# Queries and keys with 14 tokens a partition, turned in 64x64 blocks; values in four transfers a unit

## The chip, the cores and the metric

One Trainium2 chip, one of its cores. The metric is the device time of one execution in microseconds. Three runs of the kernel before took 314.25, 314.24 and 313.91 us, a median of 314.24. Engines: TensorE (PE, with PEld for its weight loads), VectorE (DVE), ScalarE (ACT), GpSimd (POOL) and SyncE (SP, which only issues transfers here). POOL issues transfers too, and those convert float32 to bfloat16 on the way.

## The reference

```python
batch, n_heads, seq, head_dim = (8, 12, 448, 64)          # q, k, v: float32, 0.1 * randn
N, D, E, S_per_e, F = (3584, 768, 8, 4, 1024)             # phi [768, 32], w1 [8, 768, 1024], w2 [8, 1024, 768]

def _attn_ref(q, k, v):
    scale = 1.0 / np.sqrt(q.shape[-1])
    scores = scale * np.matmul(q, k.transpose(0, 1, 3, 2))
    m = np.max(scores, axis=-1, keepdims=True)
    e = np.exp(scores - m)
    attn = e / (np.sum(e, axis=-1, keepdims=True) + np.exp(-m) + 1e-09)
    return np.matmul(attn, v)

def _moe_ref(x, phi, w1, w2):
    logits = x @ phi
    d = np.exp(logits - logits.max(0, keepdims=True))
    d /= d.sum(0, keepdims=True) + 1e-09
    slot_input = (d.T @ x).reshape(E, S_per_e, D)
    for e in range(E):
        slot_out[e] = np.maximum(slot_input[e] @ w1[e], 0.0) @ w2[e]
    c = np.exp(logits - logits.max(1, keepdims=True))
    c /= c.sum(1, keepdims=True) + 1e-09
    return c @ slot_out.reshape(n_slots, D)
```

The attention's output, heads side by side, is the x of the second function: 3,584 tokens of 768. The maximum m cancels out of the attention but for the 1e-09, so any value will do for it that is used in all three places alike.

## The kernel before, in words

A **unit** is two batches and two heads: 24 units (`U`), `HP` = 6 head pairs for each of `BP` = 4 batch pairs. Each unit has seven **steps** (`TB` = 7), one for every 64 (`P`) query rows of both batches. The program is written out by hand: functions are entered into a plan under a step (unit x 7 + an offset) and a place in it, and the loop at the end runs each step's places in the order small, scores, mid, value, transposed scores, end, load. `SCH` holds the offsets and places of a unit's parts, `MIX` and `FIN` those of the second function, `WAT` and `LATE` those of the weight loads. Each engine works through its instructions in that order.

Parts of a unit, with their lines:

- `load_qk` (L171, through `load`, L164): queries and keys come by four POOL transfers a unit, one for each tensor and batch, two units ahead. A batch takes 64 partitions; partition p holds tokens 7p to 7p + 6 of both heads, so a run in memory is 7 x 64 floats, 1,792 bytes. `SCH['qk']` puts them at steps 1, 2 and 6.
- `load_v` (L177): values in the same layout, float32, two SP transfers a unit (by POOL in the first unit); `stage_V` (L387) casts them to bfloat16 on POOL.
- `stage_T` (L302): PE turns queries and keys so that the head dimension lies on the partitions: 28 transposes (2 tensors x 7 tokens x 2 heads), each with 128 partitions and 64 columns in and 64 x 128 out (L326). DVE copies all of it from PSUM at once (L327). For the first unit they go a batch at a time in blocks of 64 x 64 (L315), 28 for each batch, with a DVE copy for each (L317); `T0` says when the second batch comes, `T1` when the second unit's turn comes.
- `stage_S` (L330): scores for one step, four matmuls of 64 x 64 by 448 columns, or two with 128 output rows where the step also holds attention-times-value work; DVE takes the row maxima (L347) into `M`.
- `stage_MT` (L349): the maxima are turned (L354), copied by ACT (L357), their exponential goes into `em` (L360), and POOL spreads them (L364). `MT0` is its place in the first unit.
- `stage_ST` (L370), `LAG` = 11 steps later: the maxima (L375) and the transposed scores (L380) are added up in PSUM; ACT takes the exponential (L384).
- `stage_AV` (L393, L409): the exponentials times the values, 65 columns with one of ones for the sum; `stage_AVout` (ACT, L419), `stage_den` (POOL, L425), `stage_N` (reciprocal on DVE, L443; products on POOL, L432), `stage_X` (turned for the second function, L483 and a copy, L485).

The second function runs in between, once per batch pair (`mixture`), and finishes after the last unit. `gate_T` (L593) turns the gates and copies them on ACT into `cT` (L598, L600), in the order of the output rows. Weights come by POOL: 48 transfers of 64 rows (L195, placed by `WAT`), and eight late ones (L204) into rooms that the attention's buffers leave free (`LATE` adds steps to the earliest ones).

PSUM has four slots of two banks each; `slot` hands them out by a rule of when each is due to be free. Waits between engines follow from which buffers are read and written.

Of the kernel before, what the change touches and what calls it, by code (L numbers as in the profile page):

```python
# [10 lines left out]
BF16 = mybir.dt.bfloat16  # L11
# [5 lines left out]
P = 64  # L17
LAG = 11
AV0 = (15, 15, 16, 17, 18, 19, 19)
SCH = {'T': (6, 'value'), 'qk': ((2, 'load'), (1, 'mid'), (6, 'end'), (6, 'value')), 'MT': (6, 'load'), 'V': (13, 'mid'), 'v': ((14, 'load'), (17, 'end')), 'AVout': (19, 'mid'), 'N': ((23, 'value'), (23, 'small')), 'X': (27, 'end'), 'mix': (28, ''), 'den': (19, 'load'), 'lp': (29, 'value'), 'last': (21, 'load'), 'Xlast': (24, 'value'), 'k1': (20, 'mid'), 'k2': (30, 'value'), 'k3': (32, 'small'), 'k4': (34, 'load'), 'Xprev': (25, 'value'), 'T0': (1, 'mid'), 'T1': (4, 'value'), 'Vlast': (12, 'end'), 'MT0': (7, 'mid')}  # L20
MIX = {'logits': (0, 'end'), 'slot_max': (5, 'load'), 'slot_exp': (5, 'load'), 'gate_logits': (6, 'value'), 'gate_max': (6, 'value'), 'slots_T': (7, 'mid'), 'gate_exp': (7, 'value'), 'slot_sum': (13, 'small'), 'slot_in': (8, 'load'), 'gate_T': (13, 'end')}
FIN = {'merge_prev': (0, 'load'), 'logits': (1, 'load'), 'slot_max': (2, 'mid'), 'slot_exp': (2, 'value'), 'merge_max': (2, 'value'), 'slots_T': (3, 'mid'), 'slot_sum': (3, 'load'), 'merge_acc': (4, 'small'), 'slot_in': (4, 'end'), 'merge_sum': (5, 'end'), 'experts_in': (8, 'load'), 'gate_logits': (8, 'load'), 'gate_max': (9, 'small'), 'gate_exp': (10, 'load'), 'experts_hidden': (10, 'end')}
# [8 lines left out]
def kernel(  # L31
# [26 lines left out]
    G = E // 4  # L58
    scale = 1.0 / (D ** 0.5)

    ctx.enter_context(tc.manual_schedule())
    gdma = nc.gpsimd.dma_start

    const = ctx.enter_context(tc.tile_pool(name="const", bufs=1))
    small = ctx.enter_context(tc.tile_pool(name="small", bufs=2))
    psum = ctx.enter_context(tc.tile_pool(name="psum", bufs=1, space=PSUM))

    HW = (KC // 2) * F  # L70
# [817 lines left out]
```

## Time and profile before

| what | us |
|---|---|
| median of three runs | 314.24 |
| the profiled execution | 314.96 |
| its span, first to last instruction | 313.2 |
| PE, DVE, ACT, POOL busy in it | 271.0, 251.5, 209.2, 198.5 |
| DMA queue of POOL (36.69 MB), share of 16 engines' span | 70.6% |
| DMA queues of SP (21.57 MB) | 20.1% |
| granted TensorE clock, mean | 0.955 |

Busy time is the sum of what an engine executed, waiting left out. Lines of groups read: line, engine, operation, output<-input, shapes, count | busy us, mean ns of one | idle us of the engine just before them, with the work that ended it. Lines of a timeline read: start, duration, engine, line, operation, shapes, count, and in brackets the idle time before it and what ended that; "issue" is a wait for nothing that the profile shows. Groups of transfers: 112 KB each for queries and keys (96 of them, 4.4 and 4.6 us from issue to landing), 224 KB for values (46 from SP, 5.2 us), 384 KB for weights (48, 5.9 us), 768 KB for late weights (8, 8.9 us).

### The profile page before, as it was taken

The numbers are of one execution on the slowest core, as the hardware profiler recorded it, in microseconds if no ns is written. First come the engines' busy times: TensorE is split into PE (matmuls) and PEld (weight loads), VectorE is DVE, ScalarE is ACT, GpSimd is POOL, SyncE is SP. The second block draws the span as 40 slices with busy tenths as digits, with TensorE's granted clock in tenths as the row PEclk, the third lists the DMA queues.
The fourth block names the chain that finished last, engine by engine and source line by source line (L and its number), as shares of the span: only waits on it lengthen the run. The fifth ranks groups of instructions, "written<-read, shape, count | busy, mean of one in ns | idle before, by whom it ended". The sixth has DMA issues, their size and how long they took to land.

```text
span 313.2 us, 13694 instructions
## 1 busy us (share of the span) xinstructions
PE 271.0 (87%) x6080; PEld 153.6 (49%) x6080; DVE 251.5 (80%) x324; ACT 209.2 (67%) x306; POOL 198.5 (63%) x342
## 2 busy tenths in 40 slices
PE   3689899999989999998999989999989987987660
PEld 2235555655545555655555545555555553542110
DVE  2998889999979889998999889999979627328560
ACT  1127778878777888876787768787958884225351
POOL 8965877788867777798677866798756452100000
PEclk9999999999999999999999999999999999996555
DMA  6999899999989979999899889799987689936997
GB/s 89 170 166 204 164 178 171 201 179 175 176 160 178 212 136 184 190 178 176 151 201 194 164 146 200 128 207 185 196 169 162 137 143 188 210 74 268 421 425 294
DMA packets 29258, 59.12 MB, mean 189 GB/s; under 512 B 4272, under 2 KB 23216, under 8 KB 29200
## 3 DMA queue, kind: packets, MB, share of 16 engines
q0 software_dynamic: 19728, 36.69, 70.6%
q1 hardware_dynamic: 9472, 21.57, 20.1%
q8 instruction: 47, 0.77, 1.0%
q14 instruction: 11, 0.09, 0.1%
HBM read 83.46 MB, written 11.01 MB: 302 GB/s over the span
## 4 chain that ended last, share of the span: by engine, by line
PE 53%; DVE 11%; ACT 10%; DMA 9%; POOL 9%; issue 5%; ACTq 0%; POOLq 0%; DVEq 0%; SPq 0%
PE ps L409 13%; PE ps L340 11%; PE ps L375 10%; PE ps L380 7%; ACT block L384 7%; PE ps L326 5%; DVE m_sb L347 5%; DMA block<-in_moe_w_dram 4%; POOL block L167 3%; DMA out_dram<-wres 3%; PE ps L483 2%; DMA block<-in_q_dram 2%; PE ps L823 2%; DVE block L327 2%; POOL block L432 2%
## 5 line engine op out<-in xcount | busy, mean ns | idle before, releaser
L347 DVE TENSOR_REDUCE m_sb<-ps 128x2 bf16<-128x896 f32 x168 | 179.3, 1088 | 12.6 <-PE ps L340 6.0
L384 ACT ACTIVATE block<-ps 128x896 bf16<-128x896 f32 x168 | 153.5, 918 | 51.5 <-PE ps L380 44.3
L409 PE MATMUL ps<-block 64*128 64x65 bf16 (+1 forms) x2688 | 76.3, 192 | 2.1 <-issue 1.7
L409 PEld LDWEIGHTS <-block 64*128 64x128 bf16 (+1 forms) x2688 | 66.8, 97 | 20.7 <-issue 3.7
L375 PE MATMUL ps<-block 64*64 64x448 bf16 x672 | 70.0, 369 | 2.6 <-DVE acc L495 0.9
L340 PE MATMUL ps<-block 64*64 64x448 bf16 (+1 forms) x452 | 65.2, 387 | 6.2 <-DVE block L317 1.9
L380 PE MATMUL ps<-block 64*64 64x448 bf16 x672 | 66.4, 353 | 0.0
L340 PEld LDWEIGHTS <-block 64*64 64x64 bf16 (+1 forms) x452 | 23.0, 103 | 51.6 <-issue 39.8
L432 POOL TENSOR_TENSOR block<-block,rec 128x384 bf16<-128x384 f32 x46 | 37.3, 836 | 8.7 <-DVE rec L443 7.0
L375 PEld LDWEIGHTS <-block 64*64 64x64 bf16 x672 | 26.8, 106 | 13.3 <-issue 9.8
L167 POOL DMA_DIRECT2D block<-in_q_dram x48 | 30.6, 639 | 2.6 <-PE ps L340 1.8
L167 POOL DMA_DIRECT2D block<-in_k_dram x48 | 30.4, 636 | 1.9 <-PE ps L326 1.9
L364 POOL TENSOR_TENSOR block<-mt,base 128x512 bf16<-128x512 bf16 x23 | 24.2, 1054 | 6.1 <-ACT mt L357 5.9
L327 DVE COPY block<-ps 128x1792 bf16<-128x1792 bf16 x23 | 24.9, 1083 | 3.3 <-PE ps L326 3.3
L326 PE MATMUL ps<-ident,block 128*64 128x128 bf16 x644 | 24.6, 228 | 2.9 <-issue 2.7
L326 PEld LDWEIGHTS <-block 128*64 128x64 bf16 x644 | 21.6, 115 | 10.5 <-issue 9.5
L195 POOL DMA_DIRECT2D wres<-in_moe_w_dram x48 | 26.6, 556 | 0.1
L425 POOL TENSOR_TENSOR den<-block,em 128x14 f32<-128x14 f32 x23 | 4.9, 212 | 33.8 <-ACT block L419 33.2
L380 PEld LDWEIGHTS <-block 64*64 64x64 bf16 x672 | 24.2, 108 | 0.3 <-issue 0.2
L389 POOL CAST block<-block 128x896 bf16<-128x896 f32 x24 | 22.4, 933 | 2.8 <-PE ps L409 1.5
L419 ACT COPY block<-ps 128x910 f32<-128x910 f32 x22 | 20.2, 918 | 2.1 <-POOL block L437 0.6
L832 DVE TENSOR_SCALAR wres<-ps,acc 128x768 f32<-128x768 f32 (+1 forms) x16 | 14.7, 941 | 7.5 <-PE ps L823 5.0
(130 smaller groups left out, 220.4 us busy)
## 6 DMA issues: line engine op xcount, KB each, us to landing
wres<-in_moe_w_dram POOLq DMA_DIRECT2D x48, 384.0 KB, 5.9
block<-in_v_dram SPq DMA_DIRECT2D x46, 224.0 KB, 5.2
out_dram<-wres SPq DMA_DIRECT2D x11, 768.0 KB, 5.4
block<-in_moe_w_dram POOLq DMA_DIRECT2D x8, 768.0 KB, 8.9
block<-in_q_dram POOLq DMA_DIRECT2D x48, 112.0 KB, 4.4
block<-in_k_dram POOLq DMA_DIRECT2D x48, 112.0 KB, 4.6
out_dram<-wres SPq DMA_DIRECT2D x5, 384.0 KB, 5.1
block<-in_v_dram POOLq DMA_DIRECT2D x2, 224.0 KB, 4.6
```

What stands on the lines that cost most here:

```text
L167: eng.dma_start(out=t_[ds(b * P, P), :, :], in_=src[bp * 2 + b, ds(hp * 2, 2)].rearrange("h (p t) d -> p h (t d)", t=TB))
L195: gdma(out=t_[rows, ts(half, HW)], in_=src[rows, ts(half, HW)])
L326: nc.tensor.transpose(o[ds(h * D, D)], r[:, h, ts(t, D)], ident)
L327: (nc.vector.tensor_copy if OPT["T"] == "dve" else nc.scalar.copy)(t_, ps[:, :, ds(0, N2)].rearrange("p i (b n) -> p i b n", b=2))
L340: nc.tensor.matmul(ps[rs, h, ds(0, S)], QT[u][hs, b, ds(o, 128 if wide else P)], KT[u][hs, b, :], start=True, stop=True)
L347: nc.vector.tensor_reduce(m, ps[:, :, ds(0, S)], axis=AX.X, op=ALU.max)
L364: (nc.vector if end_ else nc.gpsimd).tensor_tensor(md.rearrange("p (a r n) -> p a r n", a=4, r=2), mt.rearrange("p (r n) -> p r n", r=2).u ...
L375: nc.tensor.matmul(ps[ds(b * P, P), h, ds(0, S)], select[hs, b, :], MD[u][b][hs, :], start=True, stop=False)
L380: nc.tensor.matmul(ps[ds(b * P, P), h, ds(0, S)], KT[u][hs, b, part_of(b, t)], QT[u][hs, b, :], start=False, stop=True)
L384: nc.scalar.activation(et, ps[:, :, ds(0, S)], AF.Exp, scale=scale)
L409: nc.tensor.matmul(o, et[bs, h, ds(c * 128 + b * P if c < C3 else c * 128 * (1 - b), w)], V65[u][bs, h, t, ds(0, 65)], start=(t == 0 and h ...
L432: eng.tensor_tensor(xo[:, ds(b * C3, C3)].rearrange("p c h d -> p h c d"), av[:, b, ds(0, 2 * C3 * 65)].rearrange("p (h c e) -> p h c e", ...
```

## The change

Queries and keys: one transfer for each tensor and head, still four a unit. A head takes 64 partitions, 32 for each batch; a partition holds 14 tokens, a run of 3,584 bytes. `stage_T` then works on one head's 64 partitions at a time: 56 transposes of 64 x 64, alternating between the heads, for every unit but the first. In the first unit the heads come one after the other (a call for each), queries and keys in a PSUM slot of their own, with DVE copying the queries and ACT the keys; its scores go a head at a time too, over both batches.

The tokens of a 64-row block come in another order by this (even positions, then odd ones), so values are loaded in four transfers of 32 partitions, each with every second group of seven tokens, and `gate_T` puts the output rows back in order with one ACT copy more. The plan's places, the weight loads' places and `LATE` are other ones: among them `T0` from step 1 to 0, `MT0` from (7, mid) to (5, small), `V` from (13, mid) to (13, end), the value loads a step earlier, `den` from step 19 to 20, `last` and `Xlast` a step earlier, one weight load moved from step 17 to 166.

```diff
-SCH = {..., 'V': (13, 'mid'), 'v': ((14, 'load'), (17, 'end')), ..., 'N': ((23, 'value'), (23, 'small')), ..., 'den': (19, 'load'), ..., 'last': (21, 'load'), 'Xlast': (24, 'value'), ..., 'T0': (1, 'mid'), 'T1': (4, 'value'), ..., 'MT0': (7, 'mid')}
+SCH = {..., 'V': (13, 'end'), 'v': ((13, 'load'), (16, 'end')), ..., 'N': ((23, 'small'), (23, 'small')), ..., 'den': (20, 'load'), ..., 'last': (20, 'load'), 'Xlast': (23, 'value'), ..., 'T0': (0, 'mid'), 'T1': (4, 'mid'), ..., 'MT0': (5, 'small')}
-LATE = (0, 0, 2, 0, 0, 0, 0, 0)
+LATE = (0, 0, 0, 0, 0, 1, 0, 2)
...
+    Q = P // 2
...
-    def load(u, t_, src, eng, bs):
+    def load_qk(u, which):
+        i, h = divmod(which, 2)
         bp, hp = divmod(u, HP)
+        src, name = ((q, "qr"), (k, "kr"))[i]
+        t_ = buf(*(("x", 1) if (u, i) == (1, 1) else ("raw", 2 * u + i)))
+        nc.gpsimd.dma_start(out=t_[ds(h * D, D), :],
+                            in_=src[ds(bp * 2, 2), hp * 2 + h].rearrange("b (p t) d -> b p (t d)", t=2 * TB))
+        RAW[u, name] = t_
+
+    def load_v(u, bs=range(2)):
+        bp, hp = divmod(u, HP)
+        t_ = buf("vr", 0).bitcast(F32).rearrange("p (h n) -> p h n", h=2)
         for b in bs:
-            eng.dma_start(out=t_[ds(b * P, P), :, :],
-                          in_=src[bp * 2 + b, ds(hp * 2, 2)].rearrange("h (p t) d -> p h (t d)", t=TB))
-        return t_
...
+            for r in range(2):
+                (nc.sync if u else nc.gpsimd).dma_start(
+                    out=t_[ds(b * P + r * Q, Q), :, :],
+                    in_=v[bp * 2 + b, ds(hp * 2, 2)].rearrange("h (p r t) d -> r p h (t d)", r=2, t=TB)[r])
+        RAW[u, "vr"] = t_
...
+        ps = None if u == 0 else slot([128, 2, 1024], BF16, "T")
+        for i, name in enumerate(("qr", "kr")):
+            r = RAW[u, name]
+            if u == 0:
                 ps = slot([128, 2, 1024], BF16, "T")
...
-                for h in range(2):
-                    nc.tensor.transpose(o[ds(h * D, D)], r[:, h, ts(t, D)], ident)
-        (nc.vector.tensor_copy if OPT["T"] == "dve" else nc.scalar.copy)(
-            t_, ps[:, :, ds(0, N2)].rearrange("p i (b n) -> p i b n", b=2))
+                for w in range(2):
+                    for h in hs_:
+                        hs = ds(h * D, D)
+                        nc.tensor.transpose(o[hs, :, ts(w, Q)], r[hs, ts(w * TB + t, D)], ident[hs, hs])
+            if u == 0:
+                hs = ds(hs_[0] * D, D)
+                (nc.scalar.copy if i else nc.vector.tensor_copy)(
+                    t_[hs, i], ps[hs, i, ds(0, N2)].rearrange("p (b n) -> p b n", b=2))
+        if u:
+            (nc.vector.tensor_copy if OPT["T"] == "dve" else nc.scalar.copy)(
+                t_, ps[:, :, ds(0, N2)].rearrange("p i (b n) -> p i b n", b=2))
 
     def stage_S(u, s):
         ps = slot([128, 2, 512], kind="S")
         wide = OPT["S"] == "wide" and s < 2 * C3 and u * TB + s in av_steps
+        a, c = divmod(s, C3)
+        for x in range(2):
             for r in range(1 if wide else 2):
+                h, b = (x, r if s == 2 * C3 else a) if u or s == 2 * C3 else (a, x)
+                hs, rs = ds(h * D, D), ds(0, 128) if wide else ds(r * P, P)
+                o = c * 128 + r * P + b * P if s < 2 * C3 else C3 * 128 * (1 - b)
+                nc.tensor.matmul(ps[rs, x, ds(0, S)], QT[u][hs, b, ds(o, 128 if wide else P)],
                                  KT[u][hs, b, :], start=True, stop=True)
...
-            nc.scalar.copy(cT[ds(0, 96), bp, :].rearrange("p (a b q) -> p a b q", a=2, b=2),
-                           ps[ds(0, 96)].rearrange("p b (a q) -> p a b q", a=2))
-            nc.scalar.copy(cT[ds(96, 32), bp, ds(0, 128)], ps[ds(96, 32), 0, :])
+            for a in range(2):
+                nc.scalar.copy(cT[ds(0, 96), bp, ts(a, 128)].rearrange("p (b q r) -> p b q r", b=2, r=2),
+                               ps[ds(0, 96), :, ts(a, P)].rearrange("p b (r q) -> p b q r", r=2))
+            nc.scalar.copy(cT[ds(96, 32), bp, ds(0, 128)].rearrange("p (b q r) -> p b q r", b=2, r=2),
+                           ps[ds(96, 32), 0, :].rearrange("p (b r q) -> p b q r", b=2, r=2))
```

More of the change, by code (lines that the diff above doesn't have):

```diff
@@ L21 @@
[L21 to L22 removed]
+SCH = {'T': (6, 'value'), 'qk': ((2, 'load'), (1, 'mid'), (6, 'end'), (6, 'value')), 'MT': (6, 'load'), 'V': (13, 'end'), 'v': ((13, 'load'), (16, 'end')), 'AVout': (19, 'mid'), 'N': ((23, 'small'), (23, 'small')), 'X': (27, 'end'), 'mix': (28, ''), 'den': (20, 'load'), 'lp': (29, 'value'), 'last': (20, 'load'), 'Xlast': (23, 'value'), 'k1': (20, 'mid'), 'k2': (30, 'value'), 'k3': (32, 'small'), 'k4': (34, 'load'), 'Xprev': (25, 'value'), 'T0': (0, 'mid'), 'T1': (4, 'mid'), 'Vlast': (12, 'end'), 'MT0': (5, 'small')}
```

41 lines of the change are left out of this document (8 added, 33 removed).

## The prediction, made before the changed kernel ran

> **What bounds the kernel now.** I read the page's engine row first, then the groups by line and shape, then the timeline of one unit in the steady part, of one unit that runs slower, of the first 15 us and of the tail.
>
> The page and its groups (busy us, mean ns | idle before it and who ended it):
>
> ```profile
> PE 271.0 (87%) x6080; PEld 153.6 (49%) x6080; DVE 251.5 (80%) x324; ACT 209.2 (67%) x306; POOL 198.5 (63%) x342
> q8 instruction: 47, 0.77, 1.0%
> L347 DVE TENSOR_REDUCE m_sb<-ps 128x2 bf16<-128x896 f32 x168 | 179.3, 1088 | 12.6 <-PE ps L340 6.0
> L327 DVE COPY block<-ps 128x1792 bf16<-128x1792 bf16 x23 | 24.9, 1083 | 3.3 <-PE ps L326 3.3
> ```
>
> PE looks busiest, but its ends are modelled. In the table of stretches from 26 to 248 us DVE is busy 204.8 of 222 us. One unit needs on DVE seven reductions of 1.088, the copy of the transposes 1.083, the copy of the turned result 0.616 and a reciprocal 0.230: 9.55 us. An ordinary unit takes that: the copies on line 327 start 9.51 and 9.79 us apart at 52.59, 62.10 and 71.89 us. So the middle is bound by DVE, and what counts is what makes DVE wait.
>
> Timeline of such a unit, around the transposes:
>
> ```profile
> 60.61 0.42 PE L340 MATMUL ps<-block 64*64 64x448 bf16 x4
> 61.04 0.97 PE L326 MATMUL ps<-ident,block 128*64 128x128 bf16 x28
> 62.10 1.08 DVE L327 COPY block<-ps 128x1792 bf16<-128x1792 bf16 x1
> 63.05 1.28 POOL L167 DMA_DIRECT2D block<-in_k_dram  x2
> ```
>
> The 28 transposes end at 62.01, and DVE copies at 62.10 with no idle time. Where DVE does wait for them (below, 92.31 to 92.34) it starts 0.03 us after their end, so the transposes have some 0.05 us to spare: they sit on the edge of DVE's path. The last line is the issue of two key loads for the unit after the next.
>
> A unit that is slower:
>
> ```profile
> 90.05 0.64 PE L326 MATMUL ps<-ident,block 128*64 128x128 bf16 x16
> 91.78 0.53 PE L326 MATMUL ps<-ident,block 128*64 128x128 bf16 x12 [1.09 <-issue]
> 92.34 1.09 DVE L327 COPY block<-ps 128x1792 bf16<-128x1792 bf16 x1 [1.15 <-PE ps L326]
> ```
>
> PE stops 1.09 us inside the transposes, waiting for nothing that the profile names, and DVE loses 1.15. Such stops lie a fixed count apart. Between the restarts at 85.61 and 91.77 PE runs 127 matmuls and 127 weight loads, and the same 127 and 127 between 172.89, 179.01 and 185.16. The instruction queue moved 0.77 MB in 47 packets, 16 KB each; 12,160 PE instructions over 47 are 259. So I read the stops as PE crossing from one fetched block of about 256 instructions to the next. [...]
>
> The start:
>
> ```profile
> 4.74 0.95 PE L315 MATMUL ps<-ident,block 64*64 64x64 bf16 x28 [4.74 <-DVE ident L215]
> 5.73 0.62 DVE L317 COPY block<-ps 128x896 bf16<-128x896 bf16 x1 [0.66 <-PE ps L315]
> 6.41 0.96 PE L340 MATMUL ps<-block 64*64 64x448 bf16 x8 [0.72 <-DVE block L317]
> 7.05 2.09 DVE L347 TENSOR_REDUCE m_sb<-ps 128x2 bf16<-128x896 f32 x2 [0.69 <-PE ps L340]
> ```
>
> The first reduction starts at 7.05; from there to 13.85 DVE never idles. PE is at half pace here: four score matmuls take 0.59 us before 25 us and 0.38 later, though the granted clock reads 1.00 in both. In the tail PE waits 0.94 us, at 279.36, for the last weights.
>
> **The change, part by part.** The sum is made on the profiled execution: 314.96 us, a span of 313.2 and 1.76 around it. The median is 314.24, 0.72 below; I move the median by the same sum.
>
> *First unit.* A head at a time, all 28 transposes of a head go through one quadrant of the array (rows and columns of that head). Now they alternate between two column halves: 28 in 0.95 with a mean of 0.238 for one, so (0.95 - 0.238) / 27 = 26 ns apart, two at once, 53 ns each. In one quadrant they are 53 ns apart: 27 x 0.053 + 0.24 = 1.67 us. The key half is then copied by ACT, 896 elements, nearest row 0.905 us (ACT, line 485), in place of a common DVE copy of 0.62. First scores: 4.74 + 1.67 + 0.04 + 0.905 + 0.05 = 7.41 in place of 6.41. These use two quadrants twice in place of four once, as long as the two groups at 6.41 together, 0.96. The first reduction starts near 8.4 (now 7.05). Then PE turns the second head (28 x 0.053 = 1.5 us) before the second scores, as T0 moves from step 1 to step 0: 7.41 + 0.75 + 1.5 + 0.96, second reduction near 10.65, third near 11.7 (now 9.59). That is +2.1, less about 0.2 of the 0.30 us that DVE idles at 14.15. Term **+1.9**; bounds +0.5 (first row only, ACT copy hidden by shorter load issues) and +2.6 (no idle time absorbed). MT0 moves to step 5, so PE no longer stops 2.09 us at 16.39; DVE was busy throughout, so 0. Its reductions of steps 5 and 6 must then wait for MT0's readers: copy and exponential, 0.26 + 0.23, behind the 1.08 copy of T1 on DVE, so 0 as well; without that cover 0.6.
>
> *Transposes of the other 22 units.* 56 of 64x64 in place of 28 of 128x64, alternating between two opposite quadrants. No row has this in bulk. Nearest: the first unit's 53 ns a pair at half pace, so 27 at the pace of the middle; and line 409's short ones, 64x65, in the same two quadrants, where four last 0.22 to 0.23 with 0.200 for one, some 30 ns a pair. 27 x 0.030 + 0.216 = 1.03 against 0.97: +0.06. Before them, four score matmuls last 0.42 and the transposes start only as these end. Scores and transposes will have the same 64x64 shape: between two groups of that shape (line 375 at 61.94, line 380 at 62.16) the next begins 0.22 after the first, not 0.38. So a start up to 0.09 earlier: net -0.03 to +0.06, against 0.04 to spare. Term **0**; bounds -0.9 and +1.3.
>
> *Fetched blocks.* 23 x 28 = 644 more matmuls, each with a weight load: 1,288 more PE instructions, five more blocks. Rows: line 326 lost 2.7 us to "issue" in four stops; its 23 x 56 instructions hold about five crossings, 0.54 us each. All other matmuls lost 2.6 us over some 42 crossings. A usual unit has 225 + 226 = 451 instructions; it will have 507, nearly twice 256. So a crossing keeps its place within the unit for many units. Laying the new counts over the old order puts about 15 of 53 crossings into the transposes: 15 x 0.54 = 8.1 against 2.7. The others would fall mostly where no stop is seen now, which takes back up to 2.6. Net +2.8 to +5.4; since DVE sees only part of a stop outside the transposes I take **+3.0**. Bounds: -5.3 (all stops gone) and +12 (22 x 0.54).
>
> *Gates.* Three ACT copies for two; halves of about 0.26 each replace 0.361: +0.16 us, four times. DVE has waited 1.1 us in three cases for this helper (line 600), so **+0.3**; bounds 0 and +0.6.
>
> *Loads.* 96 query and key loads have 64 rows of 3,584 bytes in place of 128 of 1,792. Issue on POOL 0.64 now, 0.556 for a weight load of 64 rows: up to 0.08 less each, but the first unit's values take two issues more (+1.25). POOL is busy 63% and its waits are hidden by DVE; its den moves behind the value cast and the key issues, past an ACT wait (33.2 us in 21 waits, up to 3.5): it feeds the reciprocal of step 23, nine microseconds later. DMA time: what is saved is the cost of half the packets; I find no stop in the middle that a late load of queries ends for more than 0.4 us, so 0 there. SP issues four value loads, not two, some 0.63 each; it waits 128.8 us for the cast on POOL, and what it loads is used a unit later. In the tail one late weight load is issued two steps earlier, two others later, and the 0.94 wait may go. Term **-0.8** for all of this; bounds -2 and +1.
>
> Sum: 1.9 + 0 + 3.0 + 0.3 - 0.8 = +4.4. Profiled 319.4; median **318.6**.
>
> **Rivals.**
>
> *Not slower: the stops leave the middle.* All crossings land among long matmuls, as the 39 or so quiet ones do now. Then the 5.3 us of stops go, DVE's 3.3 us of waits on line 326 among them: 314.2 + 1.9 - 5.3 + 0.3 - 0.8 = 310.3. It decides when fewer than about three crossings fall in the transposes. For: quiet stretches are the larger part. Against: 56 x 2 of 507 instructions are transposes, in the densest place. 21%.
>
> *Crossings at their worst.* Each of 15 costs the 1.09 that the two large ones show: 16.4 - 2.7 = +13.7, less the 2.6 that is taken back: 314.2 + 1.9 + 11.1 + 0.3 - 0.8 = 326.7. 13%.
>
> *Loads on two DMA engines.* The source's outermost dimension becomes the two batches. If a transfer were split over 2 engines, not 16: queue 0 spent 0.706 x 313.2 x 16 = 3,538 us on 36.69 MB, so 112 KB are 11 us of one engine, 0.7 us over 16 and 5.5 over two. Landing goes from 4.4 to 9.2 us. Second key load issued near 63.7, landed 72.9; its transposes run near 71.3 now, so +1.6 a unit, 21 units, and +5.7 at the start where 4.4 has to pass before the first transposes: with the other terms 314.2 + 5.2 + 33.6 + 5.7, about 359. [...] No transfer of this trace has so short an outer dimension, so no row decides. 12%.
>
> *Nothing to see.* DVE's 18.6 idle us from 8 to 248 (221.4 busy of 240) absorb the start, and the crossings stay as dear as now: 314.2. 8%.
>
> **Chances and range.** Forecast 46%, on its own 314.9 to 324. A measurement of this kernel tells 0.2% (0.6 us) from no change. Faster: the first rival and a sliver, 22%; same 7%; slower 71%. The range 310 to 328 leaves out the two-engine case and some of the two ends.
>
> **What would show it.** First reduction at 8 us or later and ACT copies in the first unit; line 326's successor near 1.03 us for 56; stops "issue" inside it in about half of the units, each with a DVE copy that waits; query loads landing near 4.4 us. Wrong if DVE's waits on the transposes shrink, or if loads land beyond 7 us.

## The result, and the profile after

The changed kernel takes 372.75 us (median of four runs, 370.98 to 376.04). The kernel before, run beside it on the same chip, takes 314.25 (four runs, 313.91 to 315.23). The ratio is 1.190, with a 95% interval of 1.183 to 1.197. Executions of one kernel fall into a faster and a slower group; ratios here compare the faster runs alone, while medians and ranges are of all runs. The forecast was 318.6 with a range of 310 to 328, so the time lies far outside it. What came is the rival "Loads on two DMA engines" (359 us), which had been given 12%.

The page of the changed kernel (profiled run 376.04 us, span 374.3): engines, DMA packets, the instruction queue, the chain that ended last by engine, two groups of DVE (busy us, mean ns | idle before and who ended it), then the DMA issues with KB and median us from issue to landing.

```profile
PE 292.6 (78%) x6722; PEld 166.3 (44%) x6724; DVE 255.8 (68%) x324; ACT 211.9 (57%) x312; POOL 207.1 (55%) x344
...
DMA packets 66928, 59.38 MB, mean 159 GB/s; under 512 B 48048, under 2 KB 60912, under 8 KB 66864
...
q8 instruction: 52, 0.85, 1.0%
...
DMA 27%; PE 27%; POOL 15%; issue 15%; DVE 10%; ACT 5%; POOLq 0%; ACTq 0%; DVEq 0%; SPq 0%
...
L347 DVE TENSOR_REDUCE m_sb<-ps 128x2 bf16<-128x896 f32 x168 | 179.8, 1090 | 28.3 <-PE ps L340 19.8
...
L328 DVE COPY block<-ps 128x1792 bf16<-128x1792 bf16 x23 | 25.1, 1091 | 28.7 <-PE ps L322 28.6
...
wres<-in_moe_w_dram POOLq DMA_DIRECT2D x48, 384.0 KB, 9.9
...
block<-in_q_dram POOLq DMA_DIRECT2D x48, 112.0 KB, 8.9
block<-in_k_dram POOLq DMA_DIRECT2D x48, 112.0 KB, 9.0
```

The same packets and chain of the kernel before:

```profile
DMA packets 29258, 59.12 MB, mean 189 GB/s; under 512 B 4272, under 2 KB 23216, under 8 KB 29200
...
PE 53%; DVE 11%; ACT 10%; DMA 9%; POOL 9%; issue 5%; ACTq 0%; POOLq 0%; DVEq 0%; SPq 0%
```

DVE has as much to do as before (255.8 us, 251.5 before) in a span that is 61 us longer: the two groups keep their mean (1,090 and 1,091 ns) and wait longer. DMA has 27% of the chain; before it had 9%, and PE 53%. Query and key transfers of the same 112 KB land after 8.9 and 9.0 us instead of 4.4 and 4.6. So do the weights, whose transfers were not changed: 9.9 instead of 5.9. The bytes are the same (59.38 MB, 59.12 before), but packets under 512 B went from 4,272 to 48,048, by 43,776. The new value transfers account for 768 of them: 48 more transfers with 16 each; the first experiment below, which has them too, counts 5,040, 768 above 4,272. The other 43,008 are 96 x 448, and 448 is 14 x 32. Each of the 96 query and key transfers has 64 rows: if two engines move 32 each, and each of the other 14 gets one small packet for every row of an engine, the count comes out exactly. The profile gives no engine numbers, so that is a reading of the count.

A line of the waits of the changed kernel (us in total, times, longest):

```profile
PE ps L322 <- DMA block<-in_k_dram: 21.3, 11, 3.3
```

L322 are the transposes, L328 DVE's copy of them, L340 and L347 the scores and their maxima. Transposes wait for keys 11 times, up to 3.3 us, and DVE waits in turn, by the groups above: 28.6 us for transposes, where it was 3.3, and 19.8 for scores, where it was 6.0.

The timeline of the changed kernel, first the start, then the transposes of an undisturbed unit and of a slower one (start us, us, engine, line, operation; in brackets the idle time before and what ended it):

```profile
9.08 1.70 PE L322 MATMUL ps<-ident,block 64*64 64x64 bf16 x28 [9.08 <-DMA block<-in_q_dram]
...
10.82 0.90 ACT L325 COPY block<-ps 64x896 bf16<-64x896 bf16 x1 [8.81 <-PE ps L322]
...
12.76 1.09 DVE L347 TENSOR_REDUCE m_sb<-ps 128x2 bf16<-128x896 f32 x1 [2.07 <-PE ps L322]
```

```profile
132.15 1.07 PE L322 MATMUL ps<-ident,block 64*64 64x64 bf16 x56
...
143.42 0.63 PE L322 MATMUL ps<-ident,block 64*64 64x64 bf16 x28
...
147.34 0.84 PE L322 MATMUL ps<-ident,block 64*64 64x64 bf16 x23 [3.29 <-DMA block<-in_k_dram]
```

The first transposes start at 9.08, not 4.74, and the first maximum comes at 12.76 instead of 7.05, 5.7 us later. At 132.15 a unit's 56 transposes run undisturbed in 1.07 us. In the next one PE turns the 28 query blocks at 143.42 and then stands until 147.34 for keys.

### The profile page after: what moved, and what is told of

Same layout as the page of the kernel before. It is cut to its first block, busy times and chain, and to the rows that moved or that the text cites. A ratio compares the mean times of both kernels' runs of the same rounds, so it can differ in the third digit from the quotient of the medians.

```text
span 374.3 us, 15011 instructions
## 1 busy us (share of the span) xinstructions
PE 292.6 (78%) x6722; PEld 166.3 (44%) x6724; DVE 255.8 (68%) x324; ACT 211.9 (57%) x312; POOL 207.1 (55%) x344
## 2 busy tenths in 40 slices
DMA packets 66928, 59.38 MB, mean 159 GB/s; under 512 B 48048, under 2 KB 60912, under 8 KB 66864
## 4 chain that ended last, share of the span: by engine, by line
DMA 27%; PE 27%; POOL 15%; issue 15%; DVE 10%; ACT 5%; POOLq 0%; ACTq 0%; DVEq 0%; SPq 0%
DMA block<-in_k_dram 21%; POOL block L170 5%; DVE m_sb L347 5%; PE ps L409 5%; PE ps L375 4%; PE ps L340 4%; PE ps L380 4%; DMA out_dram<-wres 3%; ACT block L384 3%; PE ps L647 3%; PE ps L322 3%; POOL block L389 3%; POOL block L432 3%; DMA block<-in_q_dram 3%; POOL wres L198 2%
## 5 line engine op out<-in xcount | busy, mean ns | idle before, releaser
L347 DVE TENSOR_REDUCE m_sb<-ps 128x2 bf16<-128x896 f32 x168 | 179.8, 1090 | 28.3 <-PE ps L340 19.8
L409 PE MATMUL ps<-block 64*128 64x65 bf16 (+1 forms) x2688 | 80.1, 197 | 3.3 <-issue 3.0
L375 PE MATMUL ps<-block 64*64 64x448 bf16 x672 | 77.3, 391 | 6.5 <-issue 4.2
L409 PEld LDWEIGHTS <-block 64*128 64x128 bf16 (+1 forms) x2688 | 70.2, 100 | 25.7 <-issue 10.0
L380 PE MATMUL ps<-block 64*64 64x448 bf16 x672 | 74.7, 378 | 3.9 <-issue 3.9
L340 PE MATMUL ps<-block 64*64 64x448 bf16 (+1 forms) x452 | 70.8, 405 | 8.6 <-DVE block L328 2.5
L170 POOL DMA_DIRECT2D block<-in_k_dram x48 | 32.5, 677 | 59.4 <-PE ps L322 52.6
L322 PE MATMUL ps<-ident,block 64*64 64x64 bf16 x1344 | 34.1, 204 | 34.1 <-DMA block<-in_k_dram 21.3
L340 PEld LDWEIGHTS <-block 64*64 64x64 bf16 (+1 forms) x452 | 23.7, 105 | 62.7 <-issue 53.3
L322 PEld LDWEIGHTS <-block 64*64 64x64 bf16 x1344 | 31.9, 118 | 40.1 <-DMA block<-in_k_dram 22.5
L328 DVE COPY block<-ps 128x1792 bf16<-128x1792 bf16 x23 | 25.1, 1091 | 28.7 <-PE ps L322 28.6
L375 PEld LDWEIGHTS <-block 64*64 64x64 bf16 x672 | 29.6, 109 | 16.8 <-issue 14.2
L170 POOL DMA_DIRECT2D block<-in_q_dram x48 | 35.1, 732 | 1.2 <-POOLq L874 0.8
L389 POOL CAST block<-block 128x896 bf16<-128x896 f32 x24 | 22.5, 937 | 13.9 <-DMA block<-in_v_dram 11.4
L380 PEld LDWEIGHTS <-block 64*64 64x64 bf16 x672 | 27.2, 112 | 3.9 <-issue 3.6
L485 DVE COPY block<-ps 128x896 bf16<-128x896 bf16 (+1 forms) x23 | 14.0, 610 | 9.7 <-PE ps L483 9.7
L825 PE MATMUL ps<-wres,cT 32*128 32x384 bf16 x56 | 15.0, 451 | 5.7 <-DVE wres L834 3.4
```

The source lines that it names most:

```text
L170: nc.gpsimd.dma_start(out=t_[ds(h * D, D), :], in_=src[ds(bp * 2, 2), hp * 2 + h].rearrange("b (p t) d -> b p (t d)", t=2 * TB))
L322: nc.tensor.transpose(o[hs, :, ts(w, Q)], r[hs, ts(w * TB + t, D)], ident[hs, hs])
L328: (nc.vector.tensor_copy if OPT["T"] == "dve" else nc.scalar.copy)(t_, ps[:, :, ds(0, N2)].rearrange("p i (b n) -> p i b n", b=2))
L340: nc.tensor.matmul(ps[rs, x, ds(0, S)], QT[u][hs, b, ds(o, 128 if wide else P)], KT[u][hs, b, :], start=True, stop=True)
L347: nc.vector.tensor_reduce(m, ps[:, :, ds(0, S)], axis=AX.X, op=ALU.max)
L375: nc.tensor.matmul(ps[ds(b * P, P), h, ds(0, S)], select[hs, b, :], MD[u][b][hs, :], start=True, stop=False)
```

## The experiments

Each was run beside the kernel before on the same chip, and ratios are to that. The code cuts are shortened to the lines that matter. Theory N says that the outermost dimension of two splits a transfer over two engines and no more. Theories F (the number of PE instructions and the stops between fetched blocks), P (the moved steps of the plan), U (the first unit), V (the values), T (the small transposes) and L (all but these) share out what N leaves.

**The split undone, the rest of the change kept.** Outermost in the source now are the 32 rows, so partitions hold the two batches alternately; the identity's columns are put in the order that turns them back.

```diff
-  in_=src[...].rearrange("b (p t) d -> b p (t d)", t=2 * TB))
+  in_=src[...].rearrange("b (p t) d -> p b (t d)", t=2 * TB))
+  nc.vector.tensor_copy(mixed_ident.rearrange("k (h b q) -> k h b q", h=2, b=2),
+                        ident32.rearrange("k (h q b) -> k h b q", h=2, b=2))
-  nc.tensor.transpose(o[hs, :, ts(w, Q)], r[...], ident[hs, hs])
+  nc.tensor.transpose(o[hs, :, ts(w, Q)], r[...], mixed_ident[hs, hs])
```

> The changed kernel with the two leading dimensions of the query and key source exchanged (32 runs outside, the two batches inside, so batches alternate over the partitions), and the transposes taken against an identity whose columns are in the matching order; same count, bytes and run length of the transfers. Theory N (each of these transfers runs on 2 of 16 DMA engines because its outermost dimension is 2): query and key loads land in 4.4 to 5.0 us, packets under 512 B fall from 48,048 to about 5,000, first reduction at 8 to 8.5 us, time 314 to 320 us, what the other terms of the forecast leave. Theory S (the 64x64 blocks, the first unit by heads, four value transfers or the new plan carry the loss): 360 us or more.

Measured: 323.98 us (320.61 to 324.94), ratio 1.029 [1.022, 1.036]. Its page, packets and landings:

```profile
DMA packets 23920, 59.21 MB, mean 183 GB/s; under 512 B 5040, under 2 KB 17904, under 8 KB 23856
...
block<-in_q_dram POOLq DMA_DIRECT2D x48, 112.0 KB, 4.1
block<-in_k_dram POOLq DMA_DIRECT2D x48, 112.0 KB, 4.0
```

One swap in the order of the dimensions takes back some 49 of 58 us, so theory S falls. Small packets are 4,272 + 768. But some 10 us stay, and the time lies 4 us above the range that N gave.

**The split alone, in the kernel before.** Queries and keys in two transfers each, one for each head over both batches; 1,792-byte rows, layout, transposes and plan as before.

```diff
-  for b in bs: dma_start(out=t_[ds(b * P, P), :, :], in_=src[bp * 2 + b, ds(hp * 2, 2)].rearrange("h (p t) d -> p h (t d)", t=TB))
+  dma_start(out=t_[:, h, :], in_=src[ds(bp * 2, 2), hp * 2 + h].rearrange("b (p t) d -> b p (t d)", t=TB))
```

> The kernel before with its four query and key transfers cut by head over both batches in place of by batch over both heads: same layout, same count, bytes and run length, but the source's outermost dimension is 2. Nothing else is changed. Theory N: landing 8 to 9 us, packets under 512 B up by 43,008 (96 transfers x 14 engines x 32) or by twice that if every idle engine gets as many as a busy one, first reduction near 12 us, 350 to 372 us. Theory S: 314 to 316 us.

Measured: 373.36 us (372.55 to 374.39), ratio 1.188 [1.182, 1.195], as slow as the changed kernel. From its page:

```profile
DMA packets 115274, 59.46 MB, mean 160 GB/s; under 512 B 90288, under 2 KB 109232, under 8 KB 115216
...
block<-in_q_dram POOLq DMA_DIRECT2D x48, 112.0 KB, 8.9
block<-in_k_dram POOLq DMA_DIRECT2D x48, 112.0 KB, 10.0
```

Small packets rise by 86,016 = 96 x 14 x 64: by the same reading, 128 rows over two engines are 64 each. So the outermost dimension by itself is enough for a loss as large as the whole. It doesn't add to the 10 us of the first experiment: together they would be 70, and the change costs 58. Two reasons are open: while PE stands for keys, other stops may cost nothing, and the split is not quite the same here, with twice the small packets and keys that land after 10.0 us and not 9.0.

**Only the queries, only the keys.** The same edit for one tensor at a time (0 is the queries, 1 the keys).

```diff
+  if i == 0: 
+      dma_start(out=t_[:, b], in_=src[ds(bp * 2, 2), hp * 2 + b].rearrange("b (p t) d -> b p (t d)", t=TB))
```

> As the last one, but only the queries are cut by head (outermost dimension 2); the keys stay as before. Queries are issued eleven steps ahead of use, keys seven. Theory N, with lateness of the keys as the price: about +5 us at the start and little after, 318 to 326 us. If what costs is DMA time as such (the small packets, uneven engines), half of the loss of both: 335 to 345 us. Theory S: 314 to 316 us.

> Only the keys are cut by head (outermost dimension 2); the queries stay as before. Theory N, with lateness of the keys as the price: +5 us at the start and a wait at the transposes of most units, 340 to 365 us, most of the loss of both. If DMA time as such costs: 335 to 345 us, as with queries alone. Theory S: 314 to 316 us.

Measured: queries alone 344.68 (339.81 to 349.47), ratio 1.084 [1.076, 1.092]; keys alone 348.46 (345.70 to 350.97), ratio 1.106 [1.096, 1.115]. The landings with only the queries split:

```profile
wres<-in_moe_w_dram POOLq DMA_DIRECT2D x48, 384.0 KB, 9.3
block<-in_v_dram SPq DMA_DIRECT2D x46, 224.0 KB, 7.2
...
block<-in_q_dram POOLq DMA_DIRECT2D x48, 112.0 KB, 8.4
block<-in_k_dram POOLq DMA_DIRECT2D x48, 112.0 KB, 8.1
```

The keys of this kernel are spread as before, and still land at 8.1 (4.6 before); values and weights are late too. A reading that fits is that a transfer over all engines ends only when the two that another one has filled are done; the profile names no engines, so this is not shown. What is shown is that the late transfers need not be the split ones: by this run's page keys hold 17% of the chain that ended last, values 8% and the split queries 2%. By the ratios the queries alone cost some 26 us and the keys alone some 33.

**One transfer for each batch.** The changed kernel with eight query and key transfers a unit, each of 32 rows, and nothing else changed.

```diff
-  nc.gpsimd.dma_start(out=t_[ds(h * D, D), :], in_=src[ds(bp * 2, 2), hp * 2 + h].rearrange("b (p t) d -> b p (t d)", t=2 * TB))
+  for b in range(2):
+      nc.gpsimd.dma_start(out=t_[ds(h * D + b * Q, Q), :], in_=src[bp * 2 + b, hp * 2 + h].rearrange("(p t) d -> p (t d)", t=2 * TB))
```

> The changed kernel with each query and key transfer cut in two, one for each batch, 32 rows of 3,584 bytes; the layout in memory and all else is as in the changed kernel. The outermost dimension of the source is then 32 and not 2. Theory N (the outermost dimension sets how many DMA engines share a transfer): transfers land in 3.5 to 4.6 us and not 9, small packets fall back to about 5,000, the time is 318 to 330 although POOL issues eight a unit and not four (about 2.2 us more a unit, POOL then some 75% busy). Rival A (it is the two batches' distance in one transfer, or the head-first layout, that is slow): stays above 360. Rival B (POOL's issues become the bound): above 330, with copies of the transposes waiting for keys that were issued late though they land in 4 us.

Measured: 335.18 (334.12 to 337.80), ratio 1.067 [1.059, 1.075]. Landings on its page:

```profile
block<-in_q_dram POOLq DMA_DIRECT2D x96, 56.0 KB, 3.7
block<-in_k_dram POOLq DMA_DIRECT2D x96, 56.0 KB, 4.5
```

With 32 rows outermost they land at 3.7 and 4.5, without touching the layout: N holds and rival A falls. The time is 11 us above the first experiment's: POOL spends 97.5 us on issues of queries and keys, not 53.2, and it has 16% of the chain, not 9%. That fits a price for the issues, as in rival B, but the transposes that wait for late keys, by which B was to be known, are not in this profile; where the 11 us arise is not traced.

**The values, which SP issues.** In the kernel before, the values cut by head over both batches.

```diff
-  RAW[u, "vr"] = load(u, t_, v, nc.sync if u else nc.gpsimd, bs)
+  for h in bs:
+      (nc.sync if u else nc.gpsimd).dma_start(
+          out=t_[:, h, :], in_=v[ds(bp * 2, 2), hp * 2 + h].rearrange("b (p t) d -> b p (t d)", t=TB))
```

> The kernel before with the values' two transfers cut by head over both batches, not by batch over both heads, so that the outermost dimension of their source is the two batches; they are issued by SP and convert no type, where queries and keys are issued by POOL and converted. What they load is used a unit later, so their own lateness is hidden. Theory N (the outermost dimension sets the number of engines, whoever issues): value transfers land in 9 us or more, up to 41,000 small packets more, and because two engines a transfer are loaded unevenly the query and key transfers, though spread over 16, land later as well, 6 us and more; time 318 to 340. Rival A (only the transfers that POOL issues, or only those that convert, are split so): values land in about 4 us, time 313 to 316. Rival B (split so, but other transfers are not held up): values land late, queries and keys in 4.5, time 313 to 316.

Measured: 539.53 us (537.14 to 542.48), ratio 1.723 [1.715, 1.731]: the few engines of N, but dearer than anything expected. From its page the packets, SP's queue and the chain; then SP's queue in the kernel before; then two casts that follow each other in its timeline on POOL:

```profile
DMA packets 29222, 59.12 MB, mean 110 GB/s; under 512 B 4244, under 2 KB 23192, under 8 KB 29164
...
q1 hardware_dynamic: 8828, 21.56, 10.7%
...
DMA 80%; POOL 7%; PE 5%; SPq 2%; DVE 2%; issue 2%; ACT 1%; POOLq 0%; DVEq 0%; ACTq 0%
```

```profile
q1 hardware_dynamic: 9472, 21.57, 20.1%
```

```profile
103.28 0.93 POOL L393 CAST block<-block 128x896 bf16<-128x896 f32 x1 [8.75 <-DMA block<-in_v_dram]
...
122.51 0.93 POOL L393 CAST block<-block 128x896 bf16<-128x896 f32 x1 [9.11 <-DMA block<-in_v_dram]
```

The values have one buffer: the cast must free it before the next load, so a unit can't be shorter than load plus cast. The first of these casts ends at 104.21 and the next starts at 122.51: 18.3 us for two transfers of 224 KB, and POOL, done with its other work, waits 9.11 us for them. The expectation called the lateness hidden; a use that comes a unit later hides nothing beyond a unit. Queries and keys, still spread, land at 6.5 and 5.4 (4.4 and 4.6 before), so rivals A and B fall.

The trace has two signs of two engines a transfer. SP's queue has 644 packets fewer, 46 x 14: each of its 46 value transfers lacks 14 small packets, as many as the count above leaves engines idle. Of their data packets one or two run at a time for 270 of the 283 us in which any runs, and never more than four; in the kernel before it is up to 21. Two transfers are issued together each time, at 104.23 and 104.78 for the second cast above, which fits both on the same two engines: the small packets that close the first come at 115.3 and 115.6, those of the second at 121.9 and 122.0.

The total of small packets hardly moves (4,244), since 616 come with the first unit's two value loads, 14 x 22 for each. POOL issues these and they stay float32, so POOL's transfers do not all convert, and one that doesn't is split as well: they land after 8.6 us, 4.6 before.

Now the 10 us that the engine split does not explain.

**The old plan.** The first experiment's kernel with the five tables of before, for example:

```diff
-  SCH = {... 'V': (13, 'end'), 'v': ((13, 'load'), (16, 'end')), ... 'T0': (0, 'mid'), ... 'MT0': (5, 'small')}
+  SCH = {... 'V': (13, 'mid'), 'v': ((14, 'load'), (17, 'end')), ... 'T0': (1, 'mid'), ... 'MT0': (7, 'mid')}
-  LATE = (0, 0, 0, 0, 0, 1, 0, 2)
+  LATE = (0, 0, 2, 0, 0, 0, 0, 0)
```

> The changed kernel with the 32 rows outermost in the source, as in the first experiment (324.0 us), and in addition with the plan of before: the steps at which transposes, values, gates, late weights and the last stage are put are all those of the kernel before. What is left of the change is the layout of queries and keys, the 56 small transposes, the first unit by heads and the four value transfers. Theory F (what is left over of the loss, some 10 us, comes with the 1,288 more PE instructions and the stops between fetched blocks): 320 to 327, stops without a named reason still about 9 to 11 us on PE. Theory P (the moved steps of the plan cost it): 314 to 318. Theory U (the first unit): the gap to before is already there at the second copy of the transposes, 2 us or more.

Measured: 323.92 (322.64 to 326.06), ratio 1.031 [1.023, 1.038], the same within the scatter as with the new plan. P falls. So does U as a full account: the first copy of line 331 starts at 14.24 (12.58 before), the second at 24.78 (23.64), so the start holds 1.1 to 1.7 us of the 10.

**The four value transfers alone**, in the kernel before, the second time with more runs.

```diff
+  for r in range(2):
+      dma_start(out=t_[ds(b * P + r * (P // 2), P // 2), :, :],
+                in_=v[bp * 2 + b, ds(hp * 2, 2)].rearrange("h (p t) d -> p h (t d)", t=TB)[ds(r * (P // 2), P // 2)])
```

> The kernel before with one change: a unit's values come in four transfers of 32 rows a head instead of two of 64, so SP issues four, the first unit's come from POOL in four. Theory V (the four value transfers carry part of what is left over): 317 or more. Theories F and P: within 1 us of before, 313 to 315, because SP waits most of its time and what it loads is used a unit later; the value transfers still land in about the time of before, since their 32 rows are outermost.

> The kernel before with a unit's values in four transfers of 32 rows a head, once more, with five rounds, because four runs came at 310 to 317 us, beside 312 to 318 of the kernel before. If the cut of the values is worth something by itself, the ratio stays below 0.995 with its interval; if the four runs were scatter, it comes to 0.995 to 1.005. Nothing in the profile names a gain: the value transfers land in 4.1 us and what they load is used a unit later.

Measured: first 312.82 (310.10 to 317.37), ratio 0.986 [0.978, 0.995], then 313.13 (310.10 to 316.82, twelve runs), ratio 0.997 [0.993, 1.000]. The gain of the first was mostly scatter: an interval from four runs that leaves out 1 did not hold. There is no loss in them, so V falls too.

**PE's order moved by half a block.** 64 tiny matmuls on zeros at the start, in the first experiment's kernel and in the kernel before.

```diff
+  for _ in range(64):
+      nc.tensor.matmul(spare, pad, pad[:, ds(0, 4)], start=True, stop=True)
```

> The first experiment (32 rows outermost, 324.0 us) with 64 tiny matmuls on zeros, four columns each, ahead of everything on PE: 128 more PE instructions, run while PE waits for the first loads. They shift every later instruction by half a block of 256. Theory F: the stops without a named reason move to other lines by half a block's worth of instructions, stay about 250 PE instructions apart, and the time moves by 2 us or more either way, or at least DVE's waits for the transposes change by 2 us. Theory P: the time stays within 1 us of 324, whatever the stops do. Were the 64 too slow to hide behind the first loads, the first reduction (8.21) would start later by that much.

> The kernel before with 64 tiny matmuls on zeros (four columns each) ahead of everything on PE: every later PE instruction moves by 128, half a block of 256. Theory F (the stops between fetched blocks lie in the middle on PE's way, and where they fall decides what they cost): the stops move to other lines, DVE's wait for the transposes leaves the two units where it is over 1 us now, and the time moves by 1 to 3 us either way. Theory of no weight on places: within 1 us of before.

Measured: 324.23 (320.33 to 327.41), ratio 1.034 [1.025, 1.044], beside 323.98 without the shift; and 311.50 (309.67 to 313.62, twelve runs) against 313.89, ratio 0.995 [0.992, 0.999]. In the first, DVE's waits for the transposes fell from 5.5 us to 1.8 and those for scores rose from 7.5 to 10.3: stops moved, and the time not beyond the scatter. In the second they fell from 3.3 us to 0.7, and the kernel is 0.5% faster than the one before. That the shift did this is not shown: the same waits are 2.3 us in the next run and 0.6 in the one with four value transfers (313.28 us), and both leave PE's instructions as they were. One and the same stop, of 1.09 us at 90.69 in the kernel before, is 1.09 in the one and absent in the other.

**Empty instructions.** Eight on PE ahead of each step's scores, in the kernel before.

```diff
+  for _ in range(8 if u else 0):
+      nc.tensor.nop(nofuse=True)
```

> The kernel before with eight empty instructions on PE ahead of the scores of each of the 161 steps after the first unit: 1,288 more PE instructions, as many as the change adds, with no work for the array, and nothing else changed. Theory F (what is left of the loss with 32 rows outermost, some 9 us, comes with the number of PE instructions): about five more fetched blocks, stops without a named reason grow from 5 us towards 10 on PE, time 318 to 325. Theory T (it comes with the transposes themselves, their shape and the order in which they write): 313 to 316.

Measured: 314.63 (312.06 to 319.04, twelve runs), ratio 0.999 [0.995, 1.003]. By its page the instruction queue fetched 47 packets as before, where 1,288 more instructions would have made 52. They were not fetched at all, and the run says nothing on F.

**The small transposes alone.** In the kernel before; each batch's blocks go to a bank of their own.

```diff
-  for h in range(2):
-      nc.tensor.transpose(o[ds(h * D, D)], r[:, h, ts(t, D)], ident)
+  for h, b in ((0, 0), (1, 1), (0, 1), (1, 0)):
+      bs = ds(b * P, P)
+      nc.tensor.transpose(ps[ds(h * D, D), b, i, part_of(b, t)], r[bs, h, ts(t, D)], ident[bs, bs])
```

> The kernel before with only the 28 transposes a unit of 128x64 replaced by 56 of 64x64, as many as in the changed kernel; queries and keys are loaded as before, each batch's half is turned into its own bank and the copy on DVE reads them in the other order; the first unit, the plan and the loads are those of before. Theory T (what is left of the loss with 32 rows outermost, some 9 us, comes with the transposes and the 1,288 more PE instructions): 319 to 325, 52 instruction packets, PE's stops without a named reason near 10 us. Theory L (it comes with the rest: the first unit by heads, the gates, the bigger rows): 313 to 316 here.

Measured: 329.51 us in six runs from 322.93 to 334.18; the kernel before took 313.46 in eleven, 311.25 to 317.18. The scatter is wide, but the fastest of the six is 5.8 us above the slowest of the eleven, and the two lowest, 322.93 and 326.60, are some 10 to 13 us above 313.3, the median of the ten lowest. The timeline of this kernel on PE, line 325 alone:

```profile
33.03 0.55 PE L325 MATMUL ps<-ident,block 64*64 64x64 bf16 x45
...
35.07 0.28 PE L325 MATMUL ps<-ident,block 64*64 64x64 bf16 x11 [1.50 <-issue]
...
54.63 0.64 PE L325 MATMUL ps<-ident,block 64*64 64x64 bf16 x56
```

Undisturbed, the 56 are faster than the 28 were: 0.64 us over four quadrants, not 0.97. The kernel is slower all the same. At 33.58 PE stops for 1.50 us in the middle of them and names no reason. Summed over the waits of PE, such stops are 16.0 us in 16 places here, 5.3 in 9 in the kernel before, and 11.7 in 14 in the first experiment. The part inside the transposes, in the kernel before, the first experiment and here (us in total, times, longest):

```profile
PE ps L326 <- issue: 2.7, 4, 1.1
```

```profile
PE ps L325 <- issue: 4.4, 4, 1.6
```

```profile
PE ps L325 <- issue: 7.3, 7, 1.6
```

So more than half of the growth lies outside the transposes: 2.6 us before, 7.3 and 8.7 in the other two. The transposes alone bring a loss as large as the one that is left over, with 52 instruction packets, as T has it; L's 313 to 316 falls. The order of quadrants and the banks are not those of the changed kernel, so the size can't be carried over exactly.

**Tiny matmuls spread over the unit**, 28 ahead of the scores, in the kernel before.

```diff
+  for _ in range((2 if wide else 1) if u else 0):
+      nc.tensor.matmul(ps[rs, h, ds(0, 4)], QT[u][hs, b, ds(o, 128 if wide else P)],
+                       KT[u][hs, b, ds(0, 4)], start=True, stop=True)
```

> The kernel before with 28 tiny matmuls a unit (four columns, each with its weight load) ahead of the scores of the steps after the first unit, which then write over them: 1,288 more PE instructions that the array does have to do. If the number of PE instructions and the five more fetched blocks carry what is left over: 52 instruction packets and 318 to 325. If not: below 317, the tiny matmuls' own time hidden behind DVE. Stops without a named reason on PE are to be read beside it: near 10 us by the first, near 5 by the second.

Measured: 324.58 (322.00 to 329.12), ratio 1.034 [1.030, 1.038]. Its instruction queue and two of its waits:

```profile
q8 instruction: 52, 0.85, 1.1%
```

```profile
DVE m_sb L350 <- PE ps L343: 17.2, 28, 2.9
...
PE ps L341 <- issue: 3.4, 3, 2.4
```

The expectation's two readings disagree: 52 packets and 324 us, but stops of PE without a reason are 6.3 us in 6 places, as before. Here DVE waits for the scores, 17.2 us where it was 6.0, since the tiny matmuls themselves (35.5 us of PE) stand ahead of these. So the number of instructions alone is not shown to cost the 10 us. What is shown is that small transposes in a dense burst can cost as much, and that PE's stops grow with them.

That the stops are waits for fetched instructions can be read in the traces. Counting matmuls and weight loads, 13 of the 14 stops of the first experiment and all 16 of the kernel with the transposes alone fall on the same count within a block of 256, number 191. In the first experiment PE resumes after each of the 14 between 2.2 and 2.5 us after the start of the latest packet of the instruction queue, and at none of the 38 quiet crossings does it go on sooner than that. By this reading a crossing costs where PE has worked off the rest of a block within those 2.2 us, and short instructions that stand close together make that likelier.

How much of the time these stops make is not shown by a run that takes them away. But in the profiled executions the two rise together: stops of 4.5, 4.7, 5.3, 6.2, 7.7, 11.4, 11.7 and 16.0 us go with 312.33, 313.28, 314.96, 315.08, 320.33, 324.37, 324.94 and 326.60 us (the kernel before shifted, with four value transfers, as it was and with empty instructions; the first experiment shifted, with the old plan and as it was; the transposes alone). The tiny matmuls (6.3, 323.90) and the eight transfers a unit (10.9, 334.12) lie above this row; they have costs of their own, named above.

## Why the prediction failed

*The loads, taken at -0.8.* This is the step that failed. The prediction wrote of DMA time that "what is saved is the cost of half the packets", and that no late load of queries ends a stop in the middle "for more than 0.4 us, so 0 there". It costed the rows of a transfer and not their order, and read the stops of a kernel whose transfers were all spread. In place of the 0 stand some 50 to 60 us: undoing the split takes back 49, and the split alone costs 60 (a ratio of 1.188; the changed kernel has 1.190).

*The rival.* Its landing was right, 9.2 us forecast, 8.9 and 9.0 measured, and the packet counts fit its mechanism. That the first maximum comes 5.7 us later, the number that the rival put on the start, is luck: it put 5.7 there on top of what the heads cost, and the loads by themselves moved the first transposes by 4.3 (9.08, 4.74 before). The 359 is 14 short. In the middle it priced lateness of the second keys alone, 1.6 us in each of 21 units; the profile has 11 waits for keys of up to 3.3 us, and the run with only the queries split shows that unsplit transfers come late too. What kept the forecast from it was the chance: the prediction said that "no row decides", and so it left a named mechanism with a price of its own at 12%. Nothing measured by then showed that an outermost dimension of 2 means two engines. The counts agree now for POOL's transfers: each query or key transfer has 14 x 32 or 14 x 64 small packets more where the outermost dimension is 2 (64 or 128 rows), and none more where it is 32 (5,040 in all, 4,272 + 768). It does not take a conversion: the first unit's values of the run with the values split stay float32, and come with 14 x 22 more each.

In the trace of that run both value transfers of a unit go together, with one or two data packets at a time for 270 of 283 us; that fits the same two engines for both. Which two they are, no profile here shows.

*First unit, +1.9.* Nearly right with loads on time: in the first experiment the first maximum is at 8.21 (near 8.4 forecast), the first copy of line 331 comes 1.4 us late and the second 0.9.

*Transposes, 0.* Forecast 1.03 us for 56, measured 1.07 undisturbed; too small to matter.

*Fetched blocks, +3.0, bounds to +12.* That the stops are crossings was read rightly, as the traces above show. Where they cost, and how much, was not. With the split undone, 10 us remain, of which the first unit is 0.9 to 1.4 us and stops without a reason on PE grew by 6.4; the rest is not traced. The prediction put 15 crossings into the transposes at 0.54 us each and took back up to 2.6 us elsewhere. In the first experiment 11 of 52 crossings fall there; four of them stop PE, for 1.1 us each, 4.4 together. Elsewhere nothing was taken back: those stops rose from 2.6 us to 7.3. "Crossings at their worst" gave 326.7, nearest to the 324 of that kernel, but with 15 stops of 1.09 in the transposes where four came, so its number is right by luck. By count most crossings of the first experiment cost nothing, 38 of 52 without a stop, but the other 14 sum to 11.7 us.

*Gates, +0.3, and the moved steps.* No run measured the gates alone. The moved steps of the plan are nothing that can be told: 323.92 with the old ones, 323.98 with the new. Nor could 0.6 us be told from no change, as the prediction had it from three runs: 28 runs of the kernel before lie between 310.36 and 318.08.

## What to carry to other kernels

Write down for each transfer which dimension lies outermost, on both sides, and keep it long: queries and keys landed after 4.4 and 4.6 us with 64 there, 4.1 and 4.0 with 32, 8.9 and 9.0 with 2 on the source's side. A rearrangement that only swaps two names made the step from 4 to 9 us here, some 49 us of the kernel's time, and the split delayed transfers that it does not touch: with only the queries split, keys landed after 8.1 us, not 4.6. Before trusting "used much later", count the buffers: with one, the load's length is a floor for the period. And short instructions in a burst were dearer here than their time on the engine, 56 transposes in 0.64 us than 28 in 0.97, and PE's stops without a named reason came to 16.0 us in 16 places with them, all at one count within a block of 256, 5.3 us in 9 before; halving blocks to double their number needs a margin of its own.

## What was not expected of the hardware

- A POOL transfer of queries or keys with an outermost dimension of 2 comes with 448 small packets more (64 rows) or 896 (128 rows), which reads as one for each of 14 engines and each row of a busy one; an SP transfer of values so split comes with none more, and with 14 fewer of its own (9,472 packets on SP's queue before, 8,828 with 46 transfers split).
- PE's granted clock is lower in the kernels in which PE waits most: 0.905 over the changed kernel's span and 0.76 with the values split, against 0.95 with 32 rows outermost. The same matmuls run slower there: the group of 64x64 by 448 on lines 375 and 379 of the two takes 391 and 432 ns, 369 before.
- After a fetch of instructions starts, PE crossed into the next block no sooner than 2.2 us later (the 51 crossings of the first experiment's trace that a fetch precedes; in the changed kernel's trace the shortest of 51 is 2.20).
- Undisturbed, four quadrants in turn do 56 transposes in 0.64 us, two in 1.07.
